# One static plan for attention, routing search and feed-forward; first layer's low parts by GpSimd subtractions, routing operands in PSUM

## Chip, cores, metric

The kernel runs on one core of one Trainium2 chip. The metric is the device time of one execution in microseconds (us).

## What is computed

Gated linear attention over B=4 batches, H=8 heads, S=768 tokens, head size 48 gives x, a matrix of 3072 tokens by 384. Then tokens are routed to 8 experts with a fixed capacity, and each token passes through the two layers of its expert:

```python
for t in range(S):                                   # attention
    state = alpha[:, :, t, :, None] * state + einsum('bhd,bhe->bhde', k[:, :, t], v[:, :, t])
    y[:, :, t] = einsum('bhd,bhde->bhe', q[:, :, t], state)
x = y.transpose(0, 2, 1, 3).reshape(3072, 384)
logits = x @ w_gate                                  # 3072 x 8
for idx in argsort(-logits.flatten()):               # routing: greedy, best pair first
    tok, e = idx // 8, idx % 8
    if assigned[tok] >= 0 or counts[e] >= 384: continue
    assigned[tok] = e; counts[e] += 1
for e in range(8):                                   # feed-forward, F = 1024
    out[assigned == e] = relu(x[assigned == e] @ w1[e]) @ w2[e]
```

## The kernel before

**Attention.** 24 calls of `step(s)` work on chunks of 128 tokens. All instructions of this stage go through a `Plan`: a list scheduler with a cost in us for every operation, a hop time between engines, and buffers that it assigns itself. It fixes the order of each engine's queue when the kernel is built (`order`, `issue`). The last operations store rows of x to `x_dram` in DRAM and leave the logits in `L`.

**Search.** The greedy routing is done as 8 successive searches, each of which finds which expert fills up next and with which token. One search (`search(i)`) has five passes over the digits of a token's key. A pass is a chain over two engines: DVE compares a digit against a table (`cmp`, L596), PE counts with 24 matmuls of 8 columns (L643, "counts"), DVE tests the counts (`g`, L644), PE multiplies by a matrix of ones (L650), DVE takes the maximum (`k`, L652) and forms the next digit (`nd`, L655). After the fifth pass the chosen expert is `es`, its number as an integer `ei`. `update(i)` removes the tokens that are now placed, gives every other token its next best expert (`m`, `key`, digits, `chu`), makes the first compare of the next search and the operand `o` of its counts. Each search needs the update before it, so the eight are one chain. `extract(i)` turns the placed tokens of expert i into the list `idx` of their 384 rows; three indirect DMAs on GpSimd's queue fetch these rows (`xr`, L791).

**Weights.** `weights(i, ei)` reads `ei` into a register and loads w1 and w2 of that expert by halves of 768 KB on the SP queue (L581 and the lines after it; 32 transfers in all).

**Feed-forward.** A product in full precision is made of three products of rounded operands (high times high, high times low, low times high). `split` makes the high parts (`w1hi`, `w2hi`) by an ACT copy, and the low parts (`w1lo`, `w2lo`) by an ACT copy times -1 (L820) and a DMA from GpSimd's queue that adds the raw weights to it (L824; 16 for w1, 16 for w2). `prep` transposes the rows on PE (L844) and splits them (`xh` on ACT, `xl` on DVE, L849). For each of the FB=8 blocks of the hidden layer `ffn1(i, q)` makes 9 matmuls of 128x384 into a PSUM bank `h` (two banks), ACT takes the ReLU to `hh` (L864), and DVE the rest to `hl` (L865). `ffn2(i, [q])` adds 9 matmuls to the three sums `y0..y2` (L880). After the last block ACT copies a sum to `yt` (L884) and GpSimd's queue stores 128 rows by an indirect DMA (L891). The two last blocks of the last expert are done together, sum by sum (`LAST_BLOCKS = 2`).

**Order.** From L548 on, the order of each engine's queue is set by the framework's scheduler from the order of the code and from priorities. The loop at the end calls `ffn1` of block n and `ffn2` of block n-2; update, search and extract run with high priority, those of the first three experts (`ROUTE_AHEAD = 3`) one right behind the other. In the first search, where PE has no other work, spare matmuls are issued between the steps (`spin_after`, `WARM_IN_ROUTE`).

Of the kernel before, what the change touches and what calls it, by code (L numbers as in the profile page):

```python
# [12 lines left out]
ROUTE_AHEAD = 3  # L13
DEBUG = None
LAST_BLOCKS = 2
WARM_UP = 10
WARM_IN_ROUTE = (6, 4, 2, 2)
# [21 lines left out]
class Plan:  # L39
# [31 lines left out]
    def order(self):  # L71
# [28 lines left out]
        while open_:  # L100
# [18 lines left out]
            free[eng] = end  # L119
# [13 lines left out]
            for j in after[i]:  # L133
                ready[j] = max(ready[j], end + (lat if ops[j][0] != eng else 0.0))
                missing[j] -= 1
                if not missing[j]:
                    open_.add(j)
# [4 lines left out]
    def issue(self):  # L142
        for i in self.order():
            self.ops[i][2]()


HOP = {"PE": 0.3, "DVE": 0.15, "ACT": 0.2, "POOL": 0.2, "SP": 2.2}
SLACK, SAME, SWITCH = 0.02, 6.0, 0.17
# [3 lines left out]
def gla_moe_kernel(ctx, tc, q, k, v, alpha, w_gate, w1, w2, out):  # L152
# [51 lines left out]
    pen = rc.tile([128, E], F32)  # L204
    asg = rc.tile([128, NU], F32)
# [3 lines left out]
    need = rc.tile([128, E], F32)  # L209
# [13 lines left out]
    def init_route(add):  # L223
# [18 lines left out]
        for x, y in ((ones_c, 1.0), (rem, float(CAP)), (pen, 0.0), (asg, 0.0)):  # L242
            a("POOL", 0.1, lambda x=x, y=y: gp.memset(x, y))
# [25 lines left out]
    psx = ctx.enter_context(tc.tile_pool(name="psx", bufs=2, space=bass.MemoryType.PSUM))  # L269
    att = ExitStack()  # L270
    ap_ = att.enter_context(tc.tile_pool(name="att", bufs=1))
    ps = att.enter_context(tc.tile_pool(name="ps", bufs=1, space=bass.MemoryType.PSUM))
# [61 lines left out]
    def step(s):  # L334
# [134 lines left out]
        def rows():  # L469
# [5 lines left out]
            if p == HP - 1:  # L475
                add("SP", 2.2, lambda: nc.sync.dma_start(
                    x_dram[4 * g * C:4 * (g + 1) * C].rearrange("(u p) d -> p u d", p=C), xg.t),
                    r=[(xg, i) for i in range(HP)])
# [71 lines left out]
    with tc.manual_schedule(**ordered):  # L550
        pl.issue()
    if DEBUG:
        DEBUG(pl)
    att.close()

    rw = ctx.enter_context(tc.tile_pool(name="route_work", bufs=2))
    wp = ctx.enter_context(tc.tile_pool(name="weights", bufs=2))
    fp = ctx.enter_context(tc.tile_pool(name="ffn", bufs=2))
    fps = ctx.enter_context(tc.tile_pool(name="ffn_ps", bufs=1, space=bass.MemoryType.PSUM))

    w1v = w1.rearrange("e (c p) f -> e p c f", p=128)
    w2v = w2.rearrange("e (c p) d -> e p c d", p=128)
    W1R, W2R, XR, IDX = {}, {}, {}, {}
# [7 lines left out]
    X = mybir.AxisListType.X  # L571
    second_half = []

    def weights(i, ei):
        ev = nc.sync.value_load(ei[0:1, 0:1], min_val=0, max_val=E - 1)
        W1R[i] = wp.tile([128, DB, F], F32, name="w1r")
        W2R[i] = wp.tile([128, FB, Dm], F32, name="w2r")

        def half(hf):
            fs = slice(hf * F // 2, (hf + 1) * F // 2)  # L580
            a = nc.sync.dma_start(W1R[i][:, :, fs], w1v[bass.ds(ev, 1), :, :, fs].rearrange("e p c f -> p (e c) f"))  # L581
            qs = slice(hf * FB // 2, (hf + 1) * FB // 2)
            b = nc.sync.dma_start(W2R[i][:, qs], w2v[bass.ds(ev, 1), :, qs].rearrange("e p c d -> p (e c) d"))
            return a, b

        half(0)
        if i:
            half(1)
        else:
            second_half.append(half)  # L590

    def compare(i, d, t, extra=0):
        nt = 2 ** BITS[t] + extra
        dst = cbuf[t % 2]
        for js in halves(i):
            nc.vector.tensor_tensor(words(dst, nt, js), keyed(d, nt, js), each(iotas[t], nt, js), op=OP.is_ge)  # L596
            yield dst, js

    def halves(i):
        return [slice(0, NU // 2), slice(NU // 2, NU)] if i == 0 else [slice(0, NU)]  # L600

    st = dict(chu=chu0, o=o0, dig=dig0)

    last_k = [None]

    def spin_after(n, *after):
        after = [x for x in after if x is not None]
        if n:
            o = fps.tile([128, CAP], F32, name="h", bufs=2)
            with ExitStack() as es_:  # L610
                for x in after:
                    es_.enter_context(tc.issue_after(x.ins))
                for _ in range(n):
                    x = nc.tensor.matmul(o, warm[:, :128], warm[:, :CAP], start=True, stop=True)
            after = [x]
        return after

    def search(i):
        chu, o, dig = st["chu"], st["o"], st["dig"]
        es = rw.tile([128, 1], F32, name="es")  # L620
        ei = rw.tile([128, 1], I32, name="ei")
        d = dig[:, 0]
        for t, bits in enumerate(BITS):
            nt = 2 ** bits
            final = t == nb - 1
            if i == 0 and t == 0:
                g = g0
            else:
                g = rw.tile([128, E], BF, name="g")
                parts = compare(i, d, t, final) if t else [(cbuf[0], js) for js in halves(i)]  # L630
                rt = fps.tile([128, 64], F32, name="rt")
                cnt = rt[:, 32:40]
                order = []
                if i == 0:
                    order = [last_k[0]] if last_k[0] else []
                if i == 1 and t == 0:
                    order = st["spin"]
                for cmp, js in parts:
                    with ExitStack() as es_:
# [116 lines left out]
    def extract(i, parts):  # L756
# [20 lines left out]
        if i == 0:  # L777
            st["hot"] = x
# [192 lines left out]
```

## Time and profile before

| what | value |
|---|---|
| median of 3 runs (lowest to highest) | 441.83 us (440.05 to 443.54) |
| time of the profiled execution | 440.52 us |
| its span in the profile | 438.8 us |
| PE busy, share of the span | 398.1 us, 91% |
| DVE, ACT, POOL busy | 276.2 us, 216.8 us, 185.0 us |
| attention, up to the last store of x | 0 to about 136.6 us |
| first search, its rows and weights | 136.6 to 170.8 us |
| feed-forward, with the other searches beside it | 170.8 to 430.85 us |
| last stores | 430.85 to 438.8 us |

PE is TensorE's matmul queue, PEld its weight loads, DVE VectorE, ACT ScalarE, POOL GpSimd, SP SyncE. POOLq and SPq are the DMA queues that GpSimd and SyncE issue to. PEclk is the clock granted to TensorE, as a share of full speed (in the line of 40 slices: in tenths). "out<-in" names what an instruction writes and reads; what stands in square brackets is how long its engine was idle before it, and what ended that.

### The profile page before, as it was taken

What the parts mean: (1) busy time and instruction counts of PE and PEld (TensorE: products, weight loads), DVE (VectorE), ACT (ScalarE), POOL (GpSimd) and SP (SyncE); (2) the same over time, 40 slices, a digit from 0 to 9 for tenths busy, and PEclk for the clock granted to TensorE, in tenths of its full rate; (3) what the DMA queues carried; (4) which work ended last, traced back from release to release, by engine and by line L of the source; (5) the groups of instructions that cost most, each with busy time, mean ns of one, the idle gap of its engine ahead of it and who ended that gap; (6) DMA issues with size and microseconds to landing.
All of it is one profiled execution on the core that took longest, in us unless ns stands there. A gap on an engine that the chain in (4) does not pass through costs nothing.

```text
span 438.8 us, 10527 instructions
## 1 busy us (share of the span) xinstructions
PE 398.1 (91%) x4148; PEld 359.3 (82%) x4148; DVE 276.2 (63%) x815; ACT 216.8 (49%) x383; POOL 185.0 (42%) x196
## 2 busy tenths in 40 slices
PE   4899999999994358999989999899999999999992
PEld 1788898878983337898978998798999999999992
DVE  5999798999963673696765875845967631322220
ACT  1266646646551043548356383543754775664311
POOL 6588777667730040125325281071171161530202
PEclk9999999999998565999998999969999999999997
DMA  8958997843022069899999999997896999995101
GB/s 294 358 167 261 320 321 221 270 147 109 4 73 72 1 197 216 174 285 220 209 319 209 225 319 221 299 222 130 277 244 149 290 293 284 252 237 100 55 0 54
DMA packets 44081, 88.87 MB, mean 203 GB/s; under 512 B 3840, under 2 KB 18176, under 8 KB 44032
## 3 DMA queue, kind: packets, MB, share of 16 engines
q0 software_dynamic: 11776, 34.61, 37.3%
q1 hardware_dynamic: 32256, 53.60, 36.6%
q8 instruction: 32, 0.52, 0.5%
q14 instruction: 17, 0.14, 0.1%
HBM read 53.59 MB, written 9.44 MB: 144 GB/s over the span
## 4 chain that ended last, share of the span: by engine, by line
PE 68%; DVE 13%; issue 9%; DMA 4%; ACT 2%; POOL 2%; POOLq 0%; SPq 0%; DVEq 0%; ACTq 0%
PE h L860 19%; PE y L880 18%; PE rt L643 6%; PE s L391 4%; PE y L442 4%; PE y L435 4%; PE xt L379 4%; PE lg L454 2%; DMA w1r<-in_moe_w_dram 2%; DMA w1lo<-w1r 2%; DVE cmp L596 2%; DVE tp L357 1%; DVE te L351 1%; PE xt L844 1%; PE st L403 1%
## 5 line engine op out<-in xcount | busy, mean ns | idle before, releaser
L865 DVE SCALAR_TENSOR_TENSOR hl<-h,hh 128x384 fp32r<-128x384 f32 x64 | 35.4, 555 | 64.8 <-ACT hh L864 64.5
L864 ACT ACTIVATE hh<-h 128x384 fp32r<-128x384 f32 x64 | 30.9, 485 | 77.4 <-PE h L860 70.2
L880 PE MATMUL y<-w2hi,hh 128*128 128x384 f32 x192 | 66.9, 348 | 1.9 <-ACT hh L864 1.9
L880 PE MATMUL y<-w2hi,hl 128*128 128x384 f32 x192 | 66.3, 346 | 0.0
L880 PE MATMUL y<-w2lo,hh 128*128 128x384 f32 x192 | 65.6, 342 | 0.0
L891 POOL DMA_INDIRECT out_dram<-yt,idx x24 | 27.6, 1150 | 60.2 <-ACT yt L884 55.1
L819 ACT ACTIVATE w1hi<-w1r 128x768 fp32r<-128x768 f32 x32 | 26.8, 839 | 48.8 <-DVE key L710 22.1
L791 POOL DMA_INDIRECT xr<-x_dram,idx x24 | 29.7, 1237 | 50.2 <-DVE val L722 30.3
L860 PE MATMUL h<-xh,w1lo 128*128 128x384 f32 x192 | 48.8, 355 | 1.0 <-DMA w1lo<-w1r 1.0
L860 PE MATMUL h<-xh,w1hi 128*128 128x384 f32 x192 | 48.6, 358 | 0.0
L860 PE MATMUL h<-xl,w1hi 128*128 128x384 f32 x192 | 48.4, 354 | 0.0
L824 POOL DMA_DIRECT2D w1lo<-w1r x16 | 22.2, 1385 | 52.1 <-ACT w1lo L820 38.2
L643 PEld LDWEIGHTS <-cmp 128*128 128x128 bf16 x816 | 30.6, 118 | 14.3 <-DVE cmp L596 11.1
L643 PE MATMUL rt<-o,cmp 128*128 128x8 bf16 x816 | 33.1, 175 | 7.4 <-DVE cmp L596 7.4
L880 PEld LDWEIGHTS y<-w2hi,hh 128*128 128x128 f32 x192 | 36.5, 190 | 2.4 <-ACT hh L864 2.2
L361 POOL TENSOR_TENSOR kh<-rk,te 128x512 f32<-128x512 f32 (+1 forms) x24 | 29.5, 1228 | 18.8 <-DVE z L371 11.5
L860 PEld LDWEIGHTS h<-xh,w1lo 128*128 128x128 f32 x192 | 35.5, 197 | 1.6 <-DMA w1lo<-w1r 1.5
L880 PEld LDWEIGHTS y<-w2hi,hl 128*128 128x128 f32 x192 | 36.6, 191 | 0.1
L880 PEld LDWEIGHTS y<-w2lo,hh 128*128 128x128 f32 x192 | 36.6, 191 | 0.0
L860 PEld LDWEIGHTS h<-xh,w1hi 128*128 128x128 f32 x192 | 35.7, 199 | 1.0 <-ACT xh L847 0.4
L824 POOL DMA_DIRECT2D w2lo<-w2r x16 | 15.7, 981 | 48.2 <-ACT w2lo L820 47.5
L860 PEld LDWEIGHTS h<-xl,w1hi 128*128 128x128 f32 x192 | 35.5, 197 | 0.2
(169 smaller groups left out, 837.4 us busy)
## 6 DMA issues: line engine op xcount, KB each, us to landing
w1r<-in_moe_w_dram SPq DMA_DIRECT2D x16, 768.0 KB, 8.6
w2r<-in_moe_w_dram SPq DMA_DIRECT2D x16, 768.0 KB, 10.7
w1lo<-w1r POOLq DMA_DIRECT2D x16, 768.0 KB, 8.8
w2lo<-w2r POOLq DMA_DIRECT2D x16, 768.0 KB, 9.0
al<-in_alpha_dram SPq DMA_DIRECT2D x24, 260.0 KB, 4.2
rk<-in_k_dram SPq DMA_DIRECT2D x24, 256.0 KB, 4.4
rq<-in_q_dram SPq DMA_DIRECT2D x24, 256.0 KB, 4.4
rv<-in_v_dram SPq DMA_DIRECT2D x24, 192.0 KB, 3.7
```

The source lines that it names most:

```text
L361: eng.tensor_tensor(out_.t[:, us].rearrange("p u c -> p (u c)"), x.t[:, lo:hi], f.t[:, lo:hi], op=OP.mult)
L379: nc.tensor.transpose(dst.t[:, u], src.t[:, u], ident)
L391: nc.tensor.matmul(sc.t[:, h, u], kh.t[hs, u], qh.t[hs, u], start=True, stop=True)
L643: nc.tensor.matmul(cnt, cmp[:, j // U, :, j % U], o[:, j], start=(j == 0), stop=(j == NU - 1))
L791: last_gather[0] = nc.gpsimd.indirect_dma_start(out=XR[i][:, b], out_offset=None, in_=x_dram, in_offset=bass.IndirectOffsetOnAxis(ap=IDX[i ...
L819: nc.scalar.activation(hi[ix_], raw_[ix_], AF.Copy)
L824: nc.gpsimd.dma_start(lo.bitcast(F32), raw_, accum_op=OP.add, max_dma_last_dim=8192)
L860: nc.tensor.matmul(o, a[:, d], x[:, d], start=(n == 0), stop=(n == 3 * DB - 1))
L864: nc.scalar.activation(hh, o, AF.Relu)
L865: nc.vector.scalar_tensor_tensor(hl, o, 0.0, hh, op0=OP.max, op1=OP.subtract)
L880: F2[i, q] = nc.tensor.matmul(Y[b], a[:, bs], w, start=(q == 0 and n == 0), stop=(q == FB - 1 and n == 2))
L891: st_ = nc.gpsimd.indirect_dma_start(out=out, out_offset=bass.IndirectOffsetOnAxis(ap=IDX[i][:, b:b + 1], axis=0), in_=yt, in_offset=None)
```

## The change

**One plan.** Search, update, extract, weights, split, prep, ffn1, ffn2 and the stores become operations of the same `Plan` as the attention. It ranks the operations that could start next by the cost of what hangs on them plus a base: 2000 for the search chain (`CHAIN`), 1900 for extract (`SIDE`), `at(i, q)` for the feed-forward block q of expert i. ROUTE_AHEAD, LAST_BLOCKS, the spare matmuls of the first search and the high priorities are gone. The plan's model of DVE is given an overlap of consecutive operations (`OVER`, `SELF`).

```diff
+HOP = {"PE": 0.3, "DVE": 0.15, "ACT": 0.2, "POOL": 0.2, "SP": 2.2}
+OVER, SELF = {"DVE": 0.09}, {"DVE": 0.035}
...
-            free[eng] = end
+            free[eng] = end - OVER.get(eng, 0.0)
...
+    CHAIN, SIDE = 2000.0, 1900.0
+    def at(i, q=0):
+        return 1000.0 - 32.0 * i - 3.6 * q
```

**Low parts.** The low parts of w1 are made by 8 GpSimd subtractions of 128x3x128 for each expert in place of 4 ACT copies and 2 adding DMAs. Those of w2 stay as they were. The raw halves have four buffers for w1 and four for w2 in place of two of whole experts. The second halves of the first expert's weights wait for that expert's rows in both kernels.

```diff
-                nc.scalar.activation(lo[ix_], raw_[ix_], AF.Copy, scale=-1.0)
...
-                nc.gpsimd.dma_start(lo.bitcast(F32), raw_, accum_op=OP.add, max_dma_last_dim=8192)
...
+                add(G_, 1.08, lambda c2=c2: nc.gpsimd.tensor_sub(l1.t[:, :, c2], r1.t[:, :, c2], h1.t[:, :, c2]),
+                    r=[r1, (h1, a)], w=[(l1, 2 * a + b)], port=True)
...
+            add(A_, 0.84, lambda q2=q2: nc.scalar.activation(l2.t[:, q2], r2.t[:, q2], AF.Copy, scale=-1.0),
+                r=[r2], w=[(l2, a)])
...
+        add(G_, 1.0, lambda: nc.gpsimd.dma_start(l2.t.bitcast(F32), r2.t, accum_op=OP.add, max_dma_last_dim=8192),
```

**PSUM.** Routing operands (`dig`, `chu`, `asg`, `m`, `ch`, `qe`, `ms`, `v1`, `pen`, `val`) are slices of one PSUM bank, which the order's rows call `z`, where they were tiles in SBUF. The feed-forward sums use the attention's PSUM tiles: the two halves of `s` are the two buffers of a block's first layer (`HB`; `h` before), `y`, `lg` and `xt` hold the three output sums (`YF`).

```diff
+    pdig = mine(0, 120).rearrange("p (t j) -> p t j", j=NU)
+    pchu, asg, pm, pch, pqe, pms, pv1 = (mine(120 + NU * j, NU) for j in range(7))
+    pen = mine(288, E)
+    pval = mine(296, NU * E).rearrange("p (j e) -> p j e", e=E)
...
+    HB = Kind([SC.tiles[0][:, h] for h in range(2)])
+    YF = [Kind([x]) for x in (YB.tiles[0], LG.tiles[0], XT.tiles[1])]
```

**Others.** The second layer's three products come in the order (hh,h2), (hl,h2), (hh,l2). The first gather of rows waits by name for the stores of x (`("xd", g)`). Two stores that follow each other directly on GpSimd's queue get a small memset between them. Each output sum of the last block is stored as it is finished, with no special order for the last blocks.

**Where instructions move.** Three places, each before and then after.

*DVE, from the last step of the first search on.* `es` is the chosen expert, `ei` the number that the weights' address is read from, `idx` the rows to gather, `hot` the table for `idx`, `cmp` a compare of the next search. Before, after `es`:

```order
L661 TENSOR_REDUCE es<-fl 128x1
L663 TENSOR_SCALAR q_2023<-nd,k 128x24
L664 TENSOR_SCALAR ei<-es 128x1
...
L774 TENSOR_TENSOR hot<-wb,iota 128x1536
L776 TENSOR_TENSOR rhs<-bk,cst 128x72
L774 TENSOR_TENSOR hot<-wb,iota 128x1536
L696 TENSOR_SCALAR oh<-pcs,k 65x1
L701 TENSOR_REDUCE m<-lw 128x24
L786 TENSOR_SCALAR idx<-xt 128x3
```

In the change, from the first compare of the second search on:

```order
L638 TENSOR_TENSOR cmp_96<-d_263,iota 128x3072
...
L691 TENSOR_SCALAR ei_220<-es_219 128x1
...
L804 TENSOR_TENSOR hot<-wb_237,iota 128x1536
L671 TENSOR_TENSOR g_244<-st,rem 128x8
L804 TENSOR_TENSOR hot<-wb_237,iota 128x1536
L677 TENSOR_REDUCE k_245<-st 128x1
L680 SCALAR_TENSOR_TENSOR nd_269<-d_263,k_245,z 128x24
L638 TENSOR_TENSOR cmp_97<-nd_269,iota_78 128x3072
L813 TENSOR_SCALAR idx_273<-xt 128x3
```

`ei`, which stood two rows behind `es`, now stands behind update(0) and a whole compare; `idx`, which stood ahead of update(0)'s `val`, now stands behind update(0) and two compares of the second search.

*DVE, from a search's decision to the next search's first counts, beside the first expert's blocks.* `hl` frees a PSUM buffer of the first layer, `o` is an operand of the counts. Before, a piece from the middle of it:

```order
L671 SCALAR_TENSOR_TENSOR cum<-ones_c,qe 128x24
L673 TENSOR_SCALAR ms<-asg,es 128x24
L677 SCALAR_TENSOR_TENSOR pen<-cl,pen 128x8
L865 SCALAR_TENSOR_TENSOR hl<-h,hh 128x384
L676 SCALAR_TENSOR_TENSOR cum<-ones_c,ms 128x24
L683 TENSOR_TENSOR lw<-L,pen 128x192
L679 CAST rts<-cum 128x2
L865 SCALAR_TENSOR_TENSOR hl<-h,hh 128x384
```

In the change, the end of such a stretch:

```order
L638 TENSOR_TENSOR cmp_96<-d_263,iota 128x3072
L735 SCALAR_TENSOR_TENSOR sel_230<-v_228,z 128x24
...
L758 SCALAR_TENSOR_TENSOR rem<-cl_224,rem 128x8
L691 TENSOR_SCALAR ei_220<-es_219 128x1
L753 TENSOR_SCALAR un_232<-z 128x24
L717 SCALAR_TENSOR_TENSOR z<-cum_223,offs_227,z 128x24
L757 TENSOR_TENSOR z<-z,un_232 128x24
L910 SCALAR_TENSOR_TENSOR hl_2118<-s,hh_2114 128x384
L760 TENSOR_TENSOR o_262<-ramp_b,z 128x192
```

In the change no `hl` stands between the decision (`es`, 24 rows ahead of the compare here) and the row just ahead of `o`; before, the first one comes ten rows behind `es`.

*PE, the same stretch.* `one` is the matmul by ones ahead of `es`, `s<-` a first-layer product of three matmuls, `y<-` a second-layer matmul, `tri` and `oh` belong to update. Before, such a piece at the first expert's blocks:

```order
L650 MATMUL rt<-g,one_87 128x8
L880 MATMUL y_2207<-w2hi,hl 128x384
L860 MATMUL h<-xh,w1hi 128x384 x3
L860 MATMUL h<-xl,w1hi 128x384 x3
L860 MATMUL h<-xh,w1lo 128x384 x3
L880 MATMUL y_2738<-w2hi,hh 128x384
L880 MATMUL y_2738<-w2lo,hh 128x384
L880 MATMUL y_2738<-w2hi,hl 128x384
L880 MATMUL y_2739<-w2hi,hh 128x384
...
L680 MATMUL rt<-rts,tri 128x2
```

In the change, from the matmul by ones to the first count of the next search:

```order
L675 MATMUL st<-g_215,one_87 128x8
L905 MATMUL s<-xh_2111,w1l_2101 128x384 x3
L905 MATMUL s<-xh_2111,w1h_2098 128x384 x3
L905 MATMUL s<-xl_2113,w1h_2098 128x384 x3
L905 MATMUL s<-xh_2111,w1l_2101 128x384 x3
...
L710 MATMUL st<-rts_225,tri 128x2
...
L711 MATMUL st<-rts_225,one_83 128x1
L733 MATMUL st<-cs_217,oh_229 128x8
L905 MATMUL s<-xh_2111,w1h_2098 128x384 x3
L668 LDWEIGHTS cmp_96
L668 MATMUL st<-o_262,cmp_96 128x8
```

Between the matmul by ones and the first count there stand 15 matmuls of the feed-forward now, the last three of which write a PSUM half that the `hl` shown above sets free; before, the second layer's matmuls stand there too.

719 lines of the change are left out of this document (370 added, 349 removed).

## Prediction

> **What bounds the kernel now.** I read the page first (busy times, 40 slices of about 11 us), then the table of stretches, then in the stretches where PE is not full its timeline and the chain of what ended last.
>
> ```profile
> span 438.8 us, 10527 instructions
> PE 398.1 (91%) x4148; PEld 359.3 (82%) x4148; DVE 276.2 (63%) x815; ACT 216.8 (49%) x383; POOL 185.0 (42%) x196
> PE   4899999999994358999989999899999999999992
> PEclk9999999999998565999998999969999999999997
> ...
> 138.00:150.00 12.00, 4.16 (x81) 3.34 (x82) 7.42 (x24) 0.00 (x0) 0.00 (x0) 0.59 0.16 56
> 150.00:170.00 20.00, 11.95 (x108) 8.53 (x108) 14.33 (x56) 7.45 (x11) 5.85 (x5) 0.59 0.61 148
> 182.00:228.00 46.00, 46.00 (x446) 42.51 (x445) 33.60 (x127) 24.07 (x39) 13.49 (x12) 1.00 0.99 253
> 228.00:236.00 8.00, 6.34 (x68) 5.32 (x66) 4.97 (x12) 8.00 (x13) 7.09 (x6) 0.79 0.92 205
> 236.00:282.00 46.00, 46.00 (x422) 42.64 (x423) 34.02 (x130) 22.42 (x38) 15.08 (x12) 1.00 1.03 251
> 282.00:294.00 12.00, 10.08 (x87) 8.97 (x86) 5.85 (x11) 7.41 (x13) 8.46 (x8) 0.72 0.95 262
> 294.00:431.00 137.00, 136.84 (x1019) 131.15 (x1016) 57.53 (x181) 70.69 (x120) 40.74 (x38) 1.00 0.75 189
> ```
>
> PE is full in slices 3 to 12 (attention) and again from slice 17 on. The rows with colons give stretch, length, then busy time of PE, PEld, DVE, ACT and POOL, and the granted clock. From 182 to 431 PE is full at clock 1.00 but for two holes, 228 to 236 and 282 to 294, where also the clock falls, to 0.79 and 0.72. So four places can give or take time: the first search (slices 13 to 16), the two holes, new waits in the full stretches, and the tail. Any wait of PE inside the full stretches goes straight into the end.
>
> ```profile
> 230.44 0.96 PE L643 MATMUL rt<-o,cmp 128*128 128x8 bf16 x24 [1.66 <-DVE cmp L596]
> 285.27 0.44 PE L880 MATMUL y<-w2hi,hh 128*128 128x384 f32 x1 [1.92 <-ACT hh L864]
> ...
> 215.85 8.35 DMA w1r<-in_moe_w_dram
> ACT w1hi L819 <- DMA w1r<-in_moe_w_dram: 16.5, 5, 6.7
> ```
>
> The holes begin with 1.66 us and 1.92 us of idle PE. The first is named a wait for a compare, but the chain view leads from it through `hl`, `hh` and the copies of `w1hi` to a weight transfer that landed at 224.2: ACT, which works in order, waited for weights (five times, 16.5 us in all) with `hh` behind it.
>
> **What the change takes away.** Raw weights now have buffers by halves, and half of the adding DMAs (16 of 32, 768 KB each) and ACT copies go. I take both holes as gone: idle 1.66 + 1.92, and the lost clock, 8 x (1.00 - 0.79) = 1.7 and 12 x (1.00 - 0.72) = 3.4. **Minus 8.7.**
>
> **First search.** Attention stays bound by PE, with the same operations in the same order to within a few rows: 0, with plus or minus 1.5 for the range. Then:
>
> ```profile
> 151.54 0.17 DVE L652 TENSOR_REDUCE k<-rt 128x1 f32<-128x8 f32 x1 [0.25 <-PE rt L650]
> 157.81 0.16 DVE L786 TENSOR_SCALAR idx<-xt 128x3 int32<-128x3 f32 x1 [0.26 <-PE xt L784]
> ...
> 160.42 1.79 DVE L596 TENSOR_TENSOR cmp<-dig,iota 128x3072 bf16<-128x3072 bf16 x1
> ...
> 167.22 1.63 PE L860 MATMUL h<-xh,w1hi 128*128 128x384 f32 x4
> ...
> 170.83 1.33 PE L860 MATMUL h<-xh,w1lo 128*128 128x384 f32 x3 [1.02 <-DMA w1lo<-w1r]
> 140.34 0.17 DVE L652 TENSOR_REDUCE k<-rt 128x1 f32<-128x8 f32 x1 [0.75 <-DMA x_dram<-xg]
> ```
>
> From the last `k` to `idx` it is 6.27 now. In the change two compares of 1.77 and some fifteen short DVE operations of about 0.13 stand ahead of `idx` as well: 5.5 more. The first wait in this stage (0.75, a DVE operation that waits for the store of x) has no cause left: minus 0.5. So `idx` comes at 157.8 + 5.5 - 0.5 = 162.8. From `idx` to the first block's matmuls it is 9.4 now, with a compare of 1.79 in between that delays `xl`; without it I take 8.6: PE starts at 171.4. The weights' address `ei` also moves, by about 6 us, to 158, and its transfer has 13 us for a landing that took 8.35 in a busy stretch, so the rows decide, not the weights. Before, the dense part began at 170.83, when the low part came, with 7 matmuls done; 9 matmuls take 1.56, a group of 24 counts 0.83 (below). The change starts 0.6 later, without these 7 matmuls (1.2), but with one group of counts more behind it (0.9 with its switch): **plus 0.9**. The spare matmuls did not hold the clock (0.59 in both stretches), so their loss costs nothing that this trace shows.
>
> ```profile
> 344.11 1.56 PE h L860 x9
> 296.84 0.83 PE rt L643 x24
> ```
>
> **New waits between searches.** A search's decision, the update and the next first compare are one chain on DVE; PE can only fill it with feed-forward work. Its length comes from the second such stretch, after the first expert's blocks:
>
> ```profile
> 244.79 0.16 DVE L652 TENSOR_REDUCE k<-rt 128x1 f32<-128x8 f32 x1
> 246.94 0.55 DVE L865 SCALAR_TENSOR_TENSOR hl<-h,hh 128x384 fp32r<-128x384 f32 x1
> 250.07 1.75 DVE L596 TENSOR_TENSOR cmp<-dig,iota 128x3072 bf16<-128x3072 bf16 x1
> 252.26 0.55 DVE L865 SCALAR_TENSOR_TENSOR hl<-h,hh 128x384 fp32r<-128x384 f32 x1
> 253.35 0.34 DVE L732 TENSOR_TENSOR o<-ramp_b,chu 128x192 bf16<-128x192 bf16 x1
> ```
>
> From `k` to `o` 8.9, of which two `hl` take 0.93 (each costs 0.46 of DVE, as the starts around it show), index work for extract 0.45 and one idle 0.44: 7.1 of chain, and with the one `hl` that the change puts there 7.5. What PE has in this time is read from the change's order. Beside the first expert's first blocks it is twelve matmuls (2.1 us) and small change to 2.6; the next three stand behind an `hl` that DVE does not reach before the end of the chain, and the counts behind these. 7.5 - 2.6 = 4.9 of idle PE. The other stretches have 5.8 to 6.8 of PE work in front of the counts: waits of 1.7, 0.7, 0.7 and 1.2; the last two stretches none. In the passes within a search PE has about 3.0 for DVE's 2.2, so nothing. **Plus 9.2.** The bounds for this term are 0 (DVE's chain hidden as now, where the stretch at 236 to 282 has PE at 46.00 of 46.00) and 12 (a chain of 8.9 as it ran). I stay with the sum, since the rows of the order fix what PE has to do there.
>
> A wait of 4.9 is longer than the 1.92 that opened the hole at 282, so I charge it the clock that the hole lost, **plus 3.4**; for the short waits nothing, and up to 1.7 in the range (the hole at 228).
>
> The Trainium skill, page "TensorE: Matmul & The Clock Gate", Part 1 ("The HAM clock gate"), lets the clock drop to half only after a whole idle window of about 3.4 us; by that, waits of 1.66 and 1.92 would have cost no clock, where the two holes show 0.79 and 0.72. Here the measurement decides; by the page the term for the holes would be 3.6 and not 8.7, the 4.9 alone would cost clock, and the sum would be 5 us higher.
>
> **ACT.** In the change's queue of ACT the copies of the next weights stand ahead of an `hh` of the first expert's second half; that weight transfer waits for the first rows. From landing times as above PE waits 1.6 there once, and up to 0.5 for each later expert, which I leave to the range. **Plus 1.6.**
>
> **GpSimd beside DVE.** 64 subtractions of 384 columns are new on POOL. A product of 512 columns took 1276 ns, so about 0.96 each, 61 us in all; POOL has room. But in the attention the two engines stop each other:
>
> ```profile
> 88.70 1.09 POOL L394 TENSOR_SCALAR_AFFINE_SELECT sm<-sm 128x1024 f32<-128x1024 f32 x1
> 88.86 0.96 DVE L501 TENSOR_SCALAR sg<-m 128x12 int32<-128x12 int32 x1
> 89.77 1.27 POOL L361 TENSOR_TENSOR qh<-rq,tp 128x512 f32<-128x512 f32 x1
> 89.86 1.20 DVE L503 TENSOR_TENSOR key<-m,sg 128x12 int32<-128x12 int32 x1
> L710 DVE TENSOR_TENSOR key<-m,sg 128x24 int32<-128x24 int32 x6 | 1.1, 177 | 0.0
> L361 POOL TENSOR_TENSOR qh<-rq,tp 128x512 f32<-128x512 f32 x22 | 28.1, 1276 | 2.2 <-DVE tp L357 1.3 <-DVE st L407 0.4 <-PE st L403 0.2
> ```
>
> A `key` of 12 columns that takes 0.177 at twice the width elsewhere took 1.20, and ended with POOL's operation. Bounds here: 0, if the plan's spacing holds or the passes' slack of 0.8 absorbs it, and 4.5, if a third of the 28 compares beside the feed-forward meet a subtraction of 0.96 halfway on average (28 / 3 x 0.48). I take **0**: each pass has slack of about that size, and most operands of the update have left SBUF. The Trainium skill, page "SBUF — State Buffer", section "Who interferes with whom", says why: DVE and GpSimd share a port pair that one of them holds alone, and a DVE operation with two SBUF inputs competes with a GpSimd operation that reads SBUF, one with a single such input does not. The rows above agree. By it the operations on the PSUM bank are free, and the compares, which read digits and table from SBUF, are not; that speaks against the subtractions and is the first rival.
>
> **Tail.** The last `yt` but two, the last matmul and the last store:
>
> ```profile
> 428.79 0.49 ACT L884 ACTIVATE yt<-y 128x384 f32<-128x384 f32 x1 [2.11 <-PE y L880]
> 430.50 0.34 PE L880 MATMUL y<-w2hi,hl 128*128 128x384 f32 x1
> 432.11 0.97 POOL L891 DMA_INDIRECT out_dram<-yt,idx  x1 [0.30 <-issue]
> ```
>
> The last matmul ends at 430.84, the last store begins 1.27 later, and from 430.84 to the end it is 8.0. Before, the three sums end about 1.04 apart (six matmuls of 0.174), so that the first two stores are out of the way. In the change they end 0.52 apart (three matmuls each), so three issues of 0.97 + 0.30, with a memset between them, stand in one row behind the first `yt`; the last one begins about 1.5 later against the last matmul. **Plus 1.5.**
>
> **Sum.** 0.9 - 8.7 + 9.2 + 3.4 + 1.6 + 0 + 1.5 = +7.9 on the profiled execution's 440.52, which lies 1.3 under the median: **448.4**. A difference of about 1% is what a measurement of this kernel can tell from none.
>
> **Rivals.**
>
> *Blocked compares.* The subtractions do meet compares, by the full bound of 4.5, and of the short waits, made longer by it, three lose clock as the hole at 228 did (1.7 each): 448.4 + 4.5 + 5.1 = 458. For it: the rows of 88.7 to 91. Against: 61 us of subtractions are under a quarter of the 260 us that they lie in. It decides where a meeting outlasts a pass's slack of 0.8.
>
> *PE covers the chain; not slower.* If DVE's chain from `k` to `o` takes 6.0 and not 7.5, each wait loses 1.5: 0.2 + 3.4 + 0 + 0 + 0 = 3.6 in place of 9.2, and with 3.4 idle I halve the clock's price: 448.4 - 5.6 - 1.7 = about 441. It decides at about 6.0, where the change breaks even. For it: operations in PSUM may start closer to each other, and the chain as it ran had foreign work in it whose share I could only estimate. Against: 17 of its operations begin between 244.79 and 246.94, one each 0.13, which leaves little to close up.
>
> *A shorter first search as well.* The weights come early, `hl` waits only once, and the first search ends earlier, since attention's last steps and the search share a plan: 3 to 4 us of the 34 us between attention (136.6, the last store of x) and dense part go on top of the rival before, 441 - 3.5 = 437.5, or with no waits left at all 441 - 3.6 - 3.5 = 434. Against: `idx` and `ei` stand later in the order, not earlier.
>
> **Chances and range.** Forecast (444 to 455) 0.46; blocked compares (455 to 464) 0.14; covered chain (437.4 to 444) 0.27; shorter first search (433 to 438) 0.13. Faster by over 1% (under 437.4): 0.15; within: 0.32; slower (over 446.3): 0.53. The range 437 to 461 leaves out about 0.1 below and 0.05 above; the forecast's own case alone is 444 to 455.
>
> **What would show it.** First search: the first 128x384 product at about 171.4, `idx` some 12 us behind the last `k` of the first search. Holes: no wait of ACT for `w1r` of over 1 us after 180. Waits: on PE's timeline a count group in the first expert's blocks that waits about 4.9 for `o`, and a clock under 0.9 behind it; four more of 0.7 to 1.7. Blocked compares: a 128x3072 compare of over 2 us. Tail: 9.5 from the last matmul to the end. I am wrong above all if the chain on DVE is shorter, or if the first weights come so late that they, not the rows, start the dense part.

## Result and the profile after

The change takes 511.49 us (509.61 to 514.15): 1.156 of the kernel before, 95% interval 1.147 to 1.165. Forecast were 448.4 and a range of 437 to 461. Since chips differ by some per cent between sessions, the runs below are compared by their ratio to the kernel before on the same chip; 1% is 4.4 us. Runs more than 1.5% above the fastest of their kernel stay out of the ratios, and as the traces of e1 and e6 are of such runs, their idle times are not compared with others.

From the page of the change (span, busy times, the slices) and its table of stretches (columns as in the prediction):

```profile
span 507.9 us, 10573 instructions
PE 412.1 (81%) x4134; PEld 366.4 (72%) x4134; DVE 301.6 (59%) x823; ACT 194.4 (38%) x351; POOL 229.4 (45%) x257
PE   4899999999832486995978868897869959889792
PEclk8799999999965559996999989899889989989997
...
30.00:140.00 110.00, 105.47 (x1618) 90.56 (x1614) 84.40 (x205) 59.04 (x124) 70.84 (x59) 1.00 0.57 182
140.00:177.00 37.00, 13.15 (x219) 10.65 (x219) 25.90 (x95) 6.15 (x10) 6.81 (x7) 0.56 0.28 86
177.00:300.00 123.00, 99.91 (x869) 88.90 (x869) 84.16 (x225) 45.66 (x75) 55.20 (x55) 0.87 0.56 158
300.00:398.00 98.00, 84.33 (x694) 76.12 (x694) 63.56 (x201) 36.02 (x59) 36.65 (x36) 0.92 0.48 142
398.00:498.00 100.00, 88.25 (x522) 84.45 (x521) 20.59 (x43) 36.48 (x64) 35.86 (x42) 0.97 0.40 113
```

Over none of the three stretches of the feed-forward (177 to 498) is PE full now, not even behind 398, where no search is left. The first and the last product of the feed-forward, and the tail:

```profile
177.16 2.29 PE L905 MATMUL s<-xh,w1h 128*128 128x384 f32 x6 [0.58 <-ACT xh L889]
497.66 0.34 PE L927 MATMUL lg<-w2l,hh 128*128 128x384 f32 x1
500.82 0.97 POOL L937 DMA_INDIRECT out_dram<-yo,idx  x1 [0.19 <-issue]
```

The span grew by 69.1: the first product comes 9.9 later (177.16 against 167.22), the feed-forward takes 320.8 and not 263.6 (57.2 more), the tail 9.9 and not 8.0. Summed over PE's timeline in the feed-forward, PE idles 48.3 us, where it idled 4.6: this is 43.7 of the 57.2. The other 13.5 are PE's busy time, 272.5 and not 259.0, at a mean granted clock of 0.92 and not 0.96. So the main question is what PE waits for.

### The profile page after: what moved, and what is told of

Read it like the earlier page. It is cut to its first block, busy times and chain, and to the rows that moved or that the text cites. A ratio compares the mean times of both kernels' runs of the same rounds, so it can differ in the third digit from the quotient of the medians.

```text
span 507.9 us, 10573 instructions
## 1 busy us (share of the span) xinstructions
PE 412.1 (81%) x4134; PEld 366.4 (72%) x4134; DVE 301.6 (59%) x823; ACT 194.4 (38%) x351; POOL 229.4 (45%) x257
## 4 chain that ended last, share of the span: by engine, by line
PE 48%; DVE 23%; issue 15%; DMA 5%; POOL 5%; ACT 2%; SPq 0%; POOLq 0%; DVEq 0%; ACTq 0%
PE s L905 12%; DVE cmp L638 5%; PE s L389 4%; PE y L927 4%; PE y L440 4%; PE st L668 4%; PE y L433 3%; PE xt L377 3%; PE xt L927 3%; PE lg L927 3%; DMA xr<-x_dram,idx 3%; DMA w2r<-in_moe_w_dram 3%; PE lg L452 2%; POOL out_dram L937 2%; DVE te L349 2%
## 5 line engine op out<-in xcount | busy, mean ns | idle before, releaser
L910 DVE SCALAR_TENSOR_TENSOR hl<-s,hh 128x384 fp32r<-128x384 f32 x64 | 35.3, 554 | 93.7 <-ACT hh L909 61.4
L866 POOL TENSOR_TENSOR w1l<-w1r,w1h 128x384 fp32r<-128x384 f32 x64 | 68.1, 1242 | 37.8 <-ACT w1h L861 37.7
L905 PE MATMUL s<-xh,w1h 128*128 128x384 f32 x192 | 48.7, 365 | 8.3 <-DVE hl L910 5.4
L668 PE MATMUL st<-o,cmp 128*128 128x8 bf16 x816 | 33.1, 175 | 25.1 <-DVE cmp L638 18.2
L905 PE MATMUL s<-xh,w1l 128*128 128x384 f32 x192 | 48.8, 365 | 5.4 <-DVE hl L910 3.2
L905 PE MATMUL s<-xl,w1h 128*128 128x384 f32 x192 | 49.2, 367 | 4.7 <-ACT hh L909 2.6
L638 DVE TENSOR_TENSOR cmp<-nd,iota 128x1536 bf16<-128x1536 bf16 (+4 forms) x32 | 51.5, 1619 | 0.8
L905 PEld LDWEIGHTS s<-xh,w1h 128*128 128x128 f32 x192 | 36.3, 204 | 9.7 <-DVE hl L910 5.6
L905 PEld LDWEIGHTS s<-xh,w1l 128*128 128x128 f32 x192 | 36.1, 203 | 7.6 <-issue 6.5
L905 PEld LDWEIGHTS s<-xl,w1h 128*128 128x128 f32 x192 | 36.1, 204 | 7.0 <-ACT hh L909 3.9
L389 PEld LDWEIGHTS s<-qh,kh 64*128 64x128 f32 x384 | 25.0, 195 | 11.8 <-DVE qh L359 6.5
```

The source lines that it names most:

```text
L389: nc.tensor.matmul(sc.t[:, h, u], kh.t[hs, u], qh.t[hs, u], start=True, stop=True)
L638: v_(0.12 + 0.00054 * nt * (js.stop - js.start), lambda js=js: nc.vector.tensor_tensor(words(dst, nt, js), keyed(d, nt, js), each(iotas[t] ...
L668: nc.tensor.matmul(rt[:, 32:40], dst[:, j // U, :, j % U], o[:, j], start=(j == 0), stop=(j == NU - 1))
L866: add(G_, 1.08, lambda c2=c2: nc.gpsimd.tensor_sub(l1.t[:, :, c2], r1.t[:, :, c2], h1.t[:, :, c2]), r=[r1, (h1, a)], w=[(l1, 2 * a + b)], ...
L905: nc.tensor.matmul(o.t.rearrange("p a b -> p (a b)")[:, :CAP], a.t[:, d, cs_], x.t[:, d], start=(n == 0 and d == 0), stop=(n == 2 and d == ...
L910: v_(0.553, lambda: nc.vector.scalar_tensor_tensor(hl.t, src(), 0.0, hh.t, op0=OP.max, op1=OP.subtract), r=[o, hh], w=[hl])
```

## Experiments

### What PE waits for: three mechanisms in the trace

*Compares stopped by GpSimd* (theory B in the expectations below). From the timeline of the change, POOL, DVE and PE:

```profile
288.57 7.17 POOL L866 TENSOR_TENSOR w1l<-w1r,w1h 128x384 fp32r<-128x384 f32 x7
290.32 6.23 DVE L638 TENSOR_TENSOR cmp<-nd,iota 128x1536 bf16<-128x1536 bf16 x1
296.61 0.96 PE L668 MATMUL st<-o,cmp 128*128 128x8 bf16 x24 [3.99 <-DVE cmp L638]
```

Seven subtractions run in one row; a compare that takes 0.96 alone begins in their midst, takes 6.23 and ends 0.8 behind them. It was stopped until the whole row was through.

*The halves of s wait for each other* (theory A). PE, ACT and DVE near the end, where only the feed-forward runs:

```profile
470.52 0.69 PE L905 MATMUL s<-xh,w1h 128*128 128x384 f32 x3
471.31 0.49 ACT L909 ACTIVATE hh<-s 128x384 fp32r<-128x384 f32 x1 [0.61 <-PE s L905]
471.85 0.79 PE L905 MATMUL s<-xl,w1h 128*128 128x384 f32 x3 [0.64 <-ACT hh L909]
472.73 0.56 DVE L910 SCALAR_TENSOR_TENSOR hl<-s,hh 128x384 fp32r<-128x384 f32 x1 [7.17 <-PE s L905]
473.44 0.76 PE L905 MATMUL s<-xh,w1l 128*128 128x384 f32 x3 [0.80 <-DVE hl L910]
```

The product at 470.52 belongs to the next block and writes the other half; still `hh` of this block waits for it, the next product for `hh`, `hl` for that product, and the third for `hl`. Both halves are one tile of the framework.

*DVE works the PSUM bank z one by one* (theory C). From the chain view of the change:

```profile
228.66 0.02 issue
228.68 0.18 DVE z L701
228.87 0.02 issue
228.89 0.20 DVE z L696
```

Operations on `z` begin when the one before has ended, though `pen` and `asg` have nothing to do with each other; before, such operations began 0.13 apart.

### e1 to e4: undo the shared tiles, then the subtractions

```diff
-    HB = Kind([SC.tiles[0][:, h] for h in range(2)])            # e1, e3, e4
+    HB = Kind(list(SC.tiles[0]))          # s0, s1: two tiles, ACT copies scores in two halves
-    pchu, asg, pm, pch, pqe, pms, pv1 = (mine(120 + NU * j, NU) for j in range(7))   # e2, e3, e4
+    pchu, asg, pm, pch, pqe, pms, pv1 = (rw.tile([128, NU], F32, name=...) for ...)
-                add(G_, 1.08, lambda c2=c2: nc.gpsimd.tensor_sub(l1.t[:, :, c2], ...))          # e4
+            add(A_, 0.84, lambda c=c: nc.scalar.activation(l1.t[:, :, c], r1.t[:, :, c], AF.Copy, scale=-1.0), ...)
+        add(G_, 1.4, lambda: nc.gpsimd.dma_start(l1.t.bitcast(F32), r1.t, accum_op=OP.add, ...), lat=6.0)
```

> The change, but the two PSUM halves of s are two tiles of their own (the attention then copies scores with two ACT instructions in place of one). Theory A, one tile makes every first-layer product wait for hh and hl of the block before it: the pairs of waits of 0.64 and 0.80 in the trace of the change vanish, PE's idle time from 176 to 500 falls from 48.9 us by half or more, and the time comes to 465 to 485. Theory B, compares blocked by bursts of GpSimd subtractions set the time: six compares still take 2.6 to 6.2 us and the time stays above 500. Theory C, the serial chain of DVE operations on the PSUM bank z sets the time: the waits of 2 to 4 us between searches stay, time 495 to 505.

> The change, but the routing operands that share the PSUM bank z are tiles of their own in SBUF. Theory C (every operation on z waits for the one before it, since they share a tile): from k of the last pass to the operand o the DVE chain falls from about 9.1 us to 7.5 or less, and the time by 7 to 12 us, to about 500. Theory A or B: the time changes by less than 5 us; by the port rule it may even rise, as small operations then read two SBUF operands.

> The change with both: two tiles for s, and routing operands as SBUF tiles. Theory A plus C: 450 to 470, with the blocked compares as what is left. Theory B: above 495.

> As the run before, and the low parts of w1 by an ACT copy and an adding DMA as in the kernel before, so no GpSimd subtraction. Theory A plus C with B as the remainder: no compare of 128x3072 above 1.8 us, and 5 to 15 us less than the run before, 440 to 455. Without theory B: as the run before or slower, since ACT and the DMA queues have more to do.

| run | ratio | interval |
|---|---|---|
| e1 | 1.111 | 1.104 to 1.117 |
| e2 (one run) | 1.157 | none |
| e3 | 1.125 | 1.115 to 1.135 |
| e4 | 1.048 | 1.042 to 1.054 |

A point is 1% of the kernel before. e1: the pairs of 0.64 and 0.80 are gone, worth 4.6 points, but compares of up to 7.27 us stay. With both edits (e3) the time stays above 495 us, as theory B said, and PE idles 48.7 us in the feed-forward, as in the change: what PE no longer waits for at the shared tiles, it waits for at blocked operations of DVE, up to 7.59 us at a time. Theory A is real and not the whole cause. e2: the chain is as theory C says. From `k` to the end of `o`, change and e2, on DVE's timeline:

```profile
306.02 0.17 DVE L677 TENSOR_REDUCE k<-st 128x1 f32<-128x8 f32 x1 [1.03 <-PE st L675]
314.98 0.34 DVE L760 TENSOR_TENSOR o<-ramp_b,z 128x192 bf16<-128x192 bf16 x1
...
319.29 0.17 DVE L671 TENSOR_REDUCE k<-st 128x1 f32<-128x8 f32 x1 [1.05 <-PE st L669]
326.47 0.35 DVE L754 TENSOR_TENSOR o<-ramp_b,p_chu 128x192 bf16<-128x192 bf16 x1
```

It takes 9.30 in the change and 7.53 in e2. Yet the time does not fall, though seven chains that are 1.8 shorter make 12 us. The expectation of e2 held the reason: with the routing operands in SBUF, small operations read two SBUF operands as well, and the subtractions stop these too. Group rows of `nd`, the next digit, in the change, e3 and e4:

```profile
L680 DVE SCALAR_TENSOR_TENSOR nd<-nd,k,z 128x24 bf16<-128x24 bf16 x18 | 4.3, 238 | 0.6
L677 DVE SCALAR_TENSOR_TENSOR nd<-nd,k,p_dig 128x24 bf16<-128x24 bf16 x18 | 35.1, 1948 | 0.6
L677 DVE SCALAR_TENSOR_TENSOR nd<-nd,k,p_dig 128x24 bf16<-128x24 bf16 x18 | 4.4, 244 | 0.6
```

With one operand on the PSUM bank `nd` is spared. With both in SBUF (e3) 18 of them take 31 us more, single ones up to 6.82; without subtractions (e4) they are short again. So the bank made the chain slower and at the same time kept its small operations from being stopped, and e2 and e3 undo both at once. In e2 single `nd` take up to 5.82, and compares up to 7.98.

e4, without subtractions, is 7.7 points below e3, or 34 us, over twice the 5 to 15 us that its expectation allowed; a part of this is the cost at `nd` that e3 itself had opened. Group rows of the compare of 1536 columns, change and e4:

```profile
L638 DVE TENSOR_TENSOR cmp<-nd,iota 128x1536 bf16<-128x1536 bf16 x14 | 31.2, 2233 | 0.3
L635 DVE TENSOR_TENSOR cmp<-nd,iota 128x1536 bf16<-128x1536 bf16 x14 | 13.3, 957 | 0.3
```

### e5 to e8: one part at a time, in both kernels

```diff
+                    nc.gpsimd.memset(gap, 0.0)                                   # e6, ahead of each subtraction
-                nc.scalar.activation(lo[ix_], raw_[ix_], AF.Copy, scale=-1.0)    # e7, kernel before, w1 alone
+                        nc.gpsimd.tensor_sub(lo[:, :, c_], raw_[:, :, c_], hi[:, :, c_])
+OVER, SELF = {"DVE": 0.09}, {"DVE": 0.035}                                      # e8, kernel before
```

e5 is the change with the last part of the diff above alone.

> The change with one thing undone: the low parts of w1 come by an ACT copy and an adding DMA again, with no GpSimd subtraction; one tile for s, routing operands on the PSUM bank. Theory B (the subtractions block DVE's compares and arrive late): from the 511 of the change to 470 to 485, no compare longer than 1.8 us, PE idle in the feed-forward at 20 to 28 us. Theory A plus C (shared tiles) as the main cause: 495 or more.

> The change, with a memset of one column by GpSimd ahead of each subtraction, so that two subtractions never follow each other directly. If a burst of subtractions holds the shared path from DVE because the next one is taken up before the first has ended, DVE gets in between: the longest compare falls from 6.2 us to at most 3 us, and the time by 10 to 25 us, to 486 to 500. If the path is lost for another reason (each compare has to wait until GpSimd's queue is empty), compares stay at 4 to 7 us and the time at 505 to 520.

> The kernel before, with one part of the change alone: the low parts of w1 by 8 GpSimd subtractions for each expert, in the framework's order. Theory B says that the subtractions cost by themselves: compares of 2.5 us and more beside them, 455 to 480. If they cost only in the static order of the change, where they stand in bursts behind stores that are late: within 1% of the kernel before, or faster, as the two holes of the kernel before close.

> The kernel before, with only the plan's model of DVE changed as in the change (0.09 of overlap, 0.035 to a dependent operation on the same engine), which alters the attention's order alone. If that is why attention ends later in the change (last product with the gate's weights at 139.1 and not 134.9): that product at 138 to 140 here, and the time 3 to 5 us longer. If not: within 1 us of the kernel before.

| run | ratio | interval |
|---|---|---|
| e5 | 1.127 | 1.115 to 1.138 |
| e6 (one run) | 1.117 | none |
| e7 | 1.071 | 1.062 to 1.080 |
| e8 | 1.017 | 1.010 to 1.024 |

e7 is the plainest: the subtractions alone cost the kernel before 7.1%, 31 us. POOL and DVE there:

```profile
202.51 4.25 POOL L823 TENSOR_TENSOR w1lo<-w1r,w1hi 128x384 fp32r<-128x384 f32 x4
202.45 5.93 DVE L596 TENSOR_TENSOR cmp<-nd,iota 128x3072 bf16<-128x3072 bf16 x1
```

So they need no bad order to cost. PE idles 25.4 us in e7's feed-forward where it idled 4.6, and its busy time grew by 11.8 at a mean clock of 0.92. In the change, taking them out alone (e5) gives only 3.0 points, which its expectation had put down to the shared tiles: no compare is above 1.0 us (1536 columns) or 1.8 us (3072) any more, but PE still idles 38 us, now at the chain on `z` and the halves of `s`. The causes hide behind one another: undoing the shared tiles where the subtractions are gone (e5 to e4) is worth 7.9 points, undoing the subtractions where the shared tiles are gone (e3 to e4) 7.7. Neither can be called the main one. e6 is 4.0 points below the change, in one run, yet the longest compare was still 5.62, so that what the 4.0 come from is not shown:

```profile
252.13 0.49 POOL L867 MEMSET gap<- 128x1 f32 x1
252.19 1.40 POOL L868 TENSOR_TENSOR w1l<-w1r,w1h 128x384 fp32r<-128x384 f32 x1
253.15 0.48 POOL L867 MEMSET gap<- 128x1 f32 x1
253.20 1.37 POOL L868 TENSOR_TENSOR w1l<-w1r,w1h 128x384 fp32r<-128x384 f32 x1
...
251.73 5.62 DVE L638 TENSOR_TENSOR cmp<-nd,iota 128x1536 bf16<-128x1536 bf16 x1
```

The memset lies inside the subtraction's tail, the next subtraction begins 0.4 before the last has ended, and DVE does not get in between. e8: the plan's new model of DVE changes the attention's order alone, and the last product with the gate's weights comes at 138.87 (before 134.90, change 139.08), and the whole takes 6.8 us more, where 3 to 5 were expected.

### e9 and f4: which compares are stopped

```diff
+    pd = mine(0, NU)                                 # e9: the compared digit in PSUM
+    pd = rw.tile([128, NU], F32, name="p_d")         # f4: the same digit in SBUF
```

> The change, but the digit that a compare reads lies on the PSUM bank, so that a compare has one operand in SBUF (the table) and one in PSUM; the other digits go back to SBUF. If the subtractions stop a compare because it reads two operands from SBUF, no compare is longer beside a subtraction than alone, whatever that is now (a digit in PSUM may make all compares slower, 1.75 to 3.4 us for the largest). If they stop it for another reason (its output, or the wide mode), compares of 4 us and more beside bursts remain.

> As the run whose compare reads its digit from PSUM, but with the digit as a 32-bit tile in SBUF. If the lock hangs on two SBUF operands: compares run at the slower rate (3.4 us for the largest) and some are stretched beyond that beside subtractions, to 5 us and more. If it hangs on the wide mode of the 16-bit compare: none is longer than 3.4.

Both are slower (1.191 and, one run, 1.228), as all compares run at about half the rate (1.76 for 0.96, 3.36 for 1.76). DVE and POOL of e9, then of f4:

```profile
265.94 1.76 DVE L639 TENSOR_TENSOR cmp<-z,iota 128x1536 bf16<-128x1536 f32 x1
266.09 3.36 POOL L867 TENSOR_TENSOR w1l<-w1r,w1h 128x384 fp32r<-128x384 f32 x3
...
231.78 3.32 POOL L867 TENSOR_TENSOR w1l<-w1r,w1h 128x384 fp32r<-128x384 f32 x3
232.06 4.68 DVE L639 TENSOR_TENSOR cmp<-p_d,iota 128x1536 bf16<-128x1536 f32 x1
```

With the digit in PSUM fifteen compares of e9 overlap subtractions and each takes its 1.75 to 1.77 or 3.35 to 3.36; with the digit in SBUF four of f4 are stretched, to 4.68, 2.56 and 2.51 in place of 1.76, and to 4.58 in place of 3.36. Two operands in SBUF are what stops a compare, the fast 16-bit rate is not. This is the rule of the Trainium skill, page "SBUF — State Buffer", section "Who interferes with whom", that the prediction weighed; it speaks of the lock for one instruction, and the rows show it held over a row of them. This section of the Trainium skill spares an operation with one SBUF input only outside DVE's two-port modes, a condition that the prediction left out. Some operations with one tensor operand in SBUF are stopped here too, each for about one subtraction. POOL and DVE of e7:

```profile
339.98 3.98 POOL L823 TENSOR_TENSOR w1lo<-w1r,w1hi 128x384 fp32r<-128x384 f32 x4 [1.13 <-ACT w1hi L819]
341.02 0.97 DVE L765 TENSOR_SCALAR bi<-vi 128x24 int32<-128x24 int32 x1
342.00 0.97 DVE L767 TENSOR_SCALAR wb<-wi 128x24 bf16<-128x24 int32 x1
```

Undisturbed, such an operation takes 0.17. In which mode they ran, no run here shows.

### e10 to e12, f3, g1, g2: the fixed order that is left

Without shared tiles and subtractions e4 is still 4.8% above the kernel before. The next runs build on e4.

```diff
-OVER, SELF = {"DVE": 0.09}, {"DVE": 0.035}      # e10, e11, e12, g2
+OVER, SELF = {}, {}
+        pl.base = 3000.0                        # e11, e12, f3, g1, g2: hh and hl; 2500 for ei and the first extract
-                add(G_, 1.08, lambda c2=c2: nc.gpsimd.tensor_sub(l1...))        # e12, in place of ACT and the DMA
+                add(V, 0.55, lambda c2=c2: nc.vector.tensor_sub(l1...))
-            add(G_, 1.2, fetch, ..., lat=2.0)   # g1, g2: from a gather's issue to its rows
+            add(G_, 1.2, fetch, ..., lat=4.5)
```

> The change with two tiles for s, routing operands as SBUF tiles, low parts of w1 by ACT and an adding DMA, and the plan's DVE model as before. Against the run with the same three edits and the changed model, which was 1.048 of the kernel before: the attention's last gate product at 135 and not 139.8, the first feed-forward product 4 us earlier, and the time at 1.03 of the kernel before. What is left then is the waits between searches that the prediction put at 9.2 us plus 3.4 of clock, and the tail, 1.5.

> As the run before, and the weights' address, the first expert's rows, hh and hl are ranked ahead of the search chain in the plan. If the waits between searches come from hl standing behind the chain, and the late start from idx standing behind two compares: first feed-forward product at 167 to 169 and not 173, PE idle in the feed-forward under 10 us, the time within 1% of the kernel before. If not: as the run before.

> As the run before, but the low parts of w1 are made by DVE subtractions of the same shape, not by ACT and an adding DMA. It has no lock and no adding DMA, but 64 x 0.55 = 35 us more on DVE. If DVE's chain sets the pace, 5 to 15 us slower than the run before; if it has room, as fast.

> The run with two tiles for s, routing operands in SBUF and low parts by ACT and DMA (1.048 of the kernel before, with the change's model of DVE), and on top hh, hl, the weights' address and the first expert's rows ranked ahead of the search chain. If hl standing behind the chain costs what the prediction summed (9.2 and 3.4): 1.02 to 1.03. If the order matters in ways that the sum did not hold (a table order that suits one set of durations and not another): anything from 1.02 to 1.08.

> As the run with hh, hl, address and rows ranked first (1.0625 of the kernel before), with one number of the plan changed: the time from a gather's issue to its rows goes from 2.0 to 4.5 us, since the trace shows 5.6 us from issue to landing of which 1.2 is the issue. There PE stood 17 us before transposes whose rows had not landed (6.86 and 1.06 to 3.46 later). If these waits are the remainder: no wait for rows above 1 us after the first expert, PE idle in the feed-forward 19 to under 9 us, 1.02 to 1.04 of the kernel before. If the waits only move to another place of the fixed order: idle and time as in that run.

> As the run before, with the plan's DVE model of the kernel before. If attention's 4 us come back and nothing else moves: 4 to 7 us less than the run before. With the fixed order as sensitive as it was in the earlier pair of runs (plus 29 us by the same edit), it may be slower instead.

| run | ratio | interval |
|---|---|---|
| e10 | 1.116 | 1.108 to 1.124 |
| e11 | 1.068 | 1.060 to 1.076 |
| e12 | 1.057 | 1.047 to 1.067 |
| f3 | 1.063 | 1.055 to 1.070 |
| g1 | 1.026 | 1.016 to 1.035 |
| g2 | 1.078 | 1.069 to 1.087 |

e10 missed its expectation of 1.03 widely: the old model brought attention back by 2.4 us against e4 and made the whole 6.8 points slower. In its order counts and the steps ahead of them come late (PE waits of about 3.25 and 4.07, twice each). Ranking `hh`, `hl`, the weights' address and the first expert's rows first (e11) repairs 4.8 points of it. e12 makes the same 64 subtractions on DVE itself and is no slower than e11 (1.057 against 1.068), so it is not the work of subtracting that costs. On the order of e4 the same ranking gains nothing (f3, 1.063 against 1.048; PE idles 19.1 and 18.9 us), where 1.02 to 1.03 were expected if `hl` behind the chain were the cost. The rows of f3 show what else a fixed order can get wrong:

```profile
171.50 0.87 PE L885 MATMUL xt<-ident,xr 128*128 128x128 f32 x3 [6.86 <-DMA xr<-x_dram,idx]
247.22 0.79 PE L885 MATMUL xt<-ident,xr 128*128 128x128 f32 x3 [1.77 <-DMA xr<-x_dram,idx]
...
xr<-x_dram,idx POOLq DMA_INDIRECT x24, 5.6
```

PE stands in front of transposes whose rows land 5.6 us after their issue, where the plan counted 3.2 (1.2 and 2.0). With that one number mended (g1) the idle time goes from 19.1 to 11.1 and the ratio to 1.026, the best version of the static plan here. The time is as expected; the idle time was expected under 9, and waits for rows of 2.29 and 1.45 are left. What remains lies mostly outside the feed-forward, which takes 2.2 us more than in the kernel before: the first product comes 8 us later, and from the last product to the end it takes 3.3 us more. That part of these 8 is the attention's order is likely by e8, but g2, which undoes it, got 5.2 points slower: which rows of its order do that was not found.

### f1 and f2: two parts in the kernel before

```diff
-        W1R[i] = wp.tile([128, DB, F], F32, name="w1r")                  # f1
+            W1R[i, hf] = wp.tile([128, DB, F // 2], F32, name="w1r", bufs=4)
-        o = fps.tile([128, CAP], F32, name="h", bufs=2)                  # f2
+        o = HT[:, (i * FB + q) % 2, :CAP]                                # HT: one tile of two banks
```

> The kernel before, with the raw weights in four buffers of half experts, as in the change, in place of two of whole experts. The prediction's term of minus 8.7 (both holes of the kernel before close): no hole of PE between 182 and 431, and 6 to 9 us less than the kernel before. If the holes come from the adding DMAs and the queues and not from the buffers: within 1% of the kernel before, with holes at about 228 and 282.

> The kernel before, with the two PSUM banks of h as halves of one tile, as s is in the change. If halves of one tile are ordered against each other by the framework, hh and hl wait for the first products of the next block and PE for them: repeated waits of PE of 0.6 to 0.8, PE idle up from 4.6 to 20 or more, time up by 10 to 30 us. If the waits in the change were those of its own order: within 1% of the kernel before.

f1: 0.996 (0.992 to 1.000). The holes stay; the first wait shrinks to 0.76, the second grows, and ACT still waits 3.98 and 3.61 for `w1r` ahead of them (4.87 and 2.54 before). So it is not the whole buffers that make these weights late:

```profile
283.99 0.69 PE L879 MATMUL y<-w2hi,hh 128*128 128x384 f32 x1 [2.99 <-ACT hh L863]
```

f2: 1.039 (1.033 to 1.044), 17 us for one tile in place of two, in an order that the framework makes itself. PE idles 12.9 and not 4.6, less than the 20 that was expected.

## Why the prediction was wrong

- **GpSimd beside DVE** is the step that failed first. The prediction had the mechanism, as the first rival, and took 0 with a bound of 4.5 (9.6 with the rival's clock), because a meeting was priced at half a subtraction and a pass was said to have slack of 0.8. A meeting lasts as long as the rest of the row of subtractions: it stretches a compare by up to 5.3 us in the change. The subtractions alone cost 31 us in the kernel before (e7), and 34 in the mended change (e3 to e4), there with the small operations that e3 exposes. That "61 us of subtractions are under a quarter of the 260 us that they lie in" was no argument, since they come in rows, of up to seven, directly behind gathers, stores and an adding DMA on POOL's queue. The prediction's own rows also held a sign that its rule was too narrow: `sg`, which took 0.96 beside POOL, has one tensor operand only.
- **Halves of one tile** were not seen at all, a term that the sum does not have. The prediction read from the change's order what stands where, not what the framework makes wait for what. 4.6 points in the change (e1), 3.9 in the kernel before (f2).
- **New waits between searches**: right place, wrong size. The chain was put at 7.5, which is what it takes with operands in tiles of their own (7.53 in e2); on the shared bank it takes 9.30. The rival that hoped for operations in PSUM to start closer together had the sign wrong. The waits around the five stretches, summed from 195 to 203, 229 to 237, 270 to 275, 310 to 316 and 351 to 356, are about 18 and not 9.2. The stretch with the 4.9 came out at 5.3 (1.20 and 4.11), the one with 1.7 at 4.8 (1.23, 0.25, 2.92 and 0.40), the last three at 2.3 to 2.8.
- **First search**: the first product was put at 171.4 and came at 177.16. Of the 5.8 the attention has 4.2 (139.08 against 134.90), in the step "0, with plus or minus 1.5": the model's constants were taken to move a few rows without cost, and e8 shows they do cost. `idx` came 13.7 behind the last `k` and not 11.8, by the chain on `z`: with tiles of their own (e2, e3, e4) it is 11.6 to 11.7; from `idx` to the first product it was 8.7, for which 8.6 was said.
- **Minus 8.7 for the holes**: in the change ACT's waits for `w1r` behind 180 are 1.54, 0.97 and 1.08, but its weights have 57 us longer to come. Half buffers by themselves (f1) give 1.7 of the 8.7 and leave the waits. The cause was named too early; what would close the second hole stays open.
- **Tail**: plus 1.9, with 1.5 said.
- **ACT, plus 1.6**, can't be told apart in a feed-forward full of other waits.
- **Clock**: the sum had plus 3.4 and minus 5.1, and PE's busy time grew by 13.5 at the lower clock. The price by the length of a wait does not fit: the clock was about 0.5 behind the waits of 4.11 (238 to 242), 3.99 (298 to 300) and 4.48 (380 to 382), but also behind two of 0.90 and 0.72 (326 to 328), and 1.00 behind those of 2.70, 2.00 and 1.99 (258 to 262, 276 to 280, 316 to 320). What sets it stays open here.

Without the three costs, with the landing time mended and `hh`, `hl` and the first rows ranked first, the plan lies 2.6% above the kernel before (g1). The sum lay 1.5% above it. That the two are near is no support for the sum: its minus 8.7 did not come about, and its 9.2 belongs to another order.

## What to carry to other kernels

Before moving work to GpSimd beside DVE operations that read two SBUF operands, count how long GpSimd's rows of instructions are, not how busy it is: the rest of the row is what such an operation waits for. One operand in PSUM kept an operation out of it here (`nd`, 0.24 against up to 6.82). When several causes overlap, undo them in both orders before calling one the main cause. When operands are packed into one tile, look up what the framework orders by tile, for it adds waits between parts that have nothing to do with each other. A fixed order is as good as its durations: one landing time that was 2.4 us short was worth 3.7% here.

## Unexpected in the hardware

A row of GpSimd subtractions keeps a DVE operation that reads two SBUF operands out across the ends of instructions: subtractions begin 0.4 before the one ahead has ended (e6), and a compare of 0.96 took 6.23 beside seven of them, and 5.62 with a memset between each two. Smaller operations with one SBUF operand got in after about one subtraction (0.97 for 0.17). The block goes both ways: in f4 subtractions of 1.0 last 2.4 to 4.0 where a compare stands against them. A DVE operand in PSUM ends it: a compare took its 1.76 beside three subtractions, though the 32-bit digit, in PSUM or in SBUF, costs it about half its rate, and the small `nd` took its 0.24.
